# Leaky ReLU as one Prelu on ScalarE, and the third block's probabilities turned by VectorE

## The chip, the cores and the metric

The kernel runs on one core of a Trainium2 chip. The metric is the device time of one execution in microseconds (us), taken as the median of several runs. Five engines work side by side, each with its own list of instructions, done in order: PE (TensorE, matrix products), DVE (VectorE), ACT (ScalarE), POOL (GpSimd) and SP (SyncE, which here only issues DMA transfers). An instruction at the head of a list that waits holds up everything behind it in that list.

## What is computed

Attention over chunks of 64 tokens, then two feed-forward layers with 4608 tokens each; the first has a leaky ReLU, the second a rational function.

```python
# attention: q, k, v are (8, 8, 576, 64); every chunk of 64 tokens for itself
scores = (1 / sqrt(64)) * q_c @ k_c.T
attn = exp(scores - max(scores)); attn = attn / (sum(attn) + 1e-9)
x = (attn @ v_c) as (4608, 512)

# first layer: w_in (512, 2048), w_out (2048, 512)
h = x @ w_in
x = maximum(0.01 * h, h) @ w_out

# second layer
h = x @ w_in2
P = a[0] + a[1]*h + a[2]*h*h + a[3]*h*h*h
Q = 1 + |b[0]| * |h| + |b[1]| * h*h
out = (P / (Q + 1e-6)) @ w_out2
```

## The kernel before

**Tiles.** The 4608 tokens are 9 blocks of 512 (`BLOCKS`); an attention unit `u` is 128 tokens, four units to a block, 36 in all. A step of a layer is a pair (block `i`, slice `f` of 128 of the 2048 hidden columns): `gemm1` makes the 128x512 hidden values in PSUM (`hh`, two buffers), the activation turns them into `gh` and `gl`, and `gemm2` adds their product to four PSUM accumulators (`oa`, `ob`). Values are kept as a high and a low part so that three products give almost the precision of fp32; so each `gemm1` and each `gemm2` is 12 matmuls of 128x512. `gemm2` runs two steps behind `gemm1` (`L1 = 2`).

**Weights.** They come as 64-bit words and are decoded on the chip into the high and low part `w`: two maskings (`a`, lines 260, 261), `re` on ScalarE (265), `t` (269), `sg` (273), `hi` (285), `lo` (291) on VectorE, and `cp` on ScalarE (284). The first layer's are decoded in the start-up, in pieces of 1024 columns (`f` below `WIDE` = 10) and then of 512; the second layer's during the first layer.

**Attention of a unit.** `qk` and `v` load; `S` makes the scores (PE, line 359); `mx` takes the maximum and subtracts it (DVE, 367 and 369); `ex` is Exp (ACT, 376); `nm` sums and scales (DVE, 381 to 387); `T` turns the probabilities (PE against an identity matrix, 403, into PSUM); `p` copies them out (two on ACT, 411); `PV` multiplies with `v` (PE, 420); `xh` and `xl` split the result into high and low part (ACT 431, DVE 429). Scores, turned probabilities and `PV` share the PSUM tile `at` from unit 4 on (`pa` and `pb` for units 0 to 3). In the main loop the turn is done another way: `att_turn` lets VectorE transpose blocks of 32x32 from `e` straight into `pt` (line 395, four instructions for each half of the tile).

**Activation of the first layer.** Three engines' steps: `ta` (ACT, 453) copies 0.01*h out of PSUM into `t`, `tm` (DVE, 458) takes the maximum of that and h, `gh` (ACT, 463) rounds it to the high part, `gl` (DVE, 468) subtracts.

**Order.** The order within each engine is that of the program text; only waits on data move it in time. For the first 32 steps (`NSTART`: 5 of block 0, 16 of block 1, 11 more of block 0) the text order is made by a planner: `start_ops` lists every piece with an engine, an estimated duration and what must precede it, and `ordered` puts them into one list by earliest start and then by due time (`late`). So a number in that table changes the order on every engine, the SP's list of transfers too. Units 8 to 11, the third block's, are made ready in this stretch. After it, from step 32, a plain loop runs, one unit of attention in every four steps; then the second layer.

Of the kernel before, what the change touches and what calls it, by code (L numbers as in the profile page):

```python
# [34 lines left out]
L1, L2 = 2, 3  # L35
WIDE = 10
PIECES = [(f, 0, 2) for f in range(WIDE)] + [(f, h, h + 1) for f in range(WIDE, NF) for h in range(2)]
NPAIR = 4


def start_ops():


    ops, d = [], 0.15

    def op(key, eng, us, *deps, wait=d):
        ops.append((key, eng, us, wait, [k for k in deps if k is not None]))

    last_b1 = SPLIT + NF - 1
    for u in range(13):  # L50
        first = u < NPAIR
        op(("qk", u), "Q", 1.4, ("S", u - 2), wait=2.2)
        op(("S", u), "P", 1.0, ("qk", u), ("xl", u - 2) if first else ("p", u - 1), ("xl", NPAIR - 1) if u == NPAIR else None)
        op(("mx", u), "D", 1.4, ("S", u), ("T", u - 2))
        op(("ex", u), "A", 0.63, ("mx", u))
        op(("nm", u), "D", 1.8, ("ex", u))
        op(("T", u), "P", 1.0, ("nm", u), ("p", u - 1), ("ex", u), ("xl", u - 1) if not first else None)
        op(("p", u), "A", 1.2, ("T", u), ("PV", u - 2) if u < 8 else ("PV", u - 1))
        op(("v", u), "Q", 0.7, ("PV", u - 2), wait=2.2)
        if u == 12:  # L60
            continue
        op(("PV", u), "P", 1.0, ("p", u), ("v", u), ("xl", u - (2 if first else 1)))
        op(("xh", u), "A", 0.6, ("PV", u), ("G1", last_b1) if u >= 8 else None)
        op(("xl", u), "D", 0.69, ("xh", u))
    op(("qk", 13), "Q", 1.4, ("S", 11), wait=2.2)
    for n, (f, a, b) in enumerate(PIECES):
        w = b - a
        ring = 3
        old = n - ring
        if f >= WIDE and PIECES[n - ring][0] < WIDE:  # L70
            old = None
        tail = [("lo", n - 3)]
        if f >= WIDE - 1:
            tail.append(("PV", 7))
        if f >= WIDE:
            tail += [("lo", WIDE - 1 - j) for j in range(3)]
        op(("raw", n), "Q", 1.45 * w, ("lo", old) if old is not None else None, wait=2.2)
        op(("a", n), "D", 0.1 + 0.72 * w, ("raw", n), *tail)
# [3 lines left out]
        op(("hi", n), "D", 0.07 + 0.36 * w, ("sg", n))  # L82
        op(("lo", n), "D", 0.14 + 0.55 * w, ("hi", n), ("t", n))
        op(("cp", n), "A", 0.2 + 0.4 * w, ("sg", n))
    done = {}
    for n, (f, a, b) in enumerate(PIECES):
        for h in range(a, b):
            done[f, h] = ("lo", n)
    for s, (i, f, first, last) in enumerate(STEPS[:NSTART]):
        op(("G1", s), "P", 2.72, done[f, 0], ("cp", done[f, 0][1]), *[("xl", 4 * i + k) for k in range(4)], ("tm", s - 2), ("G1", s - 1))  # L90
        op(("ta", s), "A", 0.6, ("G1", s), ("gl", s - 1))
        op(("tm", s), "D", 0.69, ("ta", s))
        op(("gh", s), "A", 0.63, ("tm", s), ("G2", s - 3))
        op(("gl", s), "D", 0.69, ("gh", s))
        if s < NSTART - L1:
            op(("G2", s), "P", 2.72, done[f, 1], ("gl", s), ("G1", s + L1 - 1), ("G2", s - 1),
               ("fin", s - 1) if first and s else ("xl", NPAIR - 1))
        if last and s < NSTART - 1:
            op(("fin", s), "A", 2.4, ("G2", s))
    return ops  # L100


def ordered(ops, log=None):
# [6 lines left out]
    for s in range(NSTART):  # L110
        late[ix["G1", s]] = 40 + step * s
        if ("G2", s) in ix:
            late[ix["G2", s]] = 40 + step * (s + L1) + 2.7
    for u in (11, 12):
        late[ix["S", u]] = 40 + step * NSTART - 60
    users = [[] for _ in ops]
    for n, dd in enumerate(deps):
        for m in dd:
# [37 lines left out]
def tile_kernel(ctx: ExitStack, tc: tile.TileContext, qt, kt, vt, w1, w2, a, b, out):  # L156
# [172 lines left out]


    ld = {}
    NTURN = 13
    NTWO = 8
    att = {}

    def load_qk(u):
# [26 lines left out]
    def att_max(u, ps):  # L363
        s = ps[:, :, 0:256].rearrange("p j (h t) -> p j h t", h=KC)
        mx = apool.tile([P, 8], F32, tag="mx", name=f"mx{u}")
        e = e0[u % 2] if u < NTWO else apool.tile([P, 8, CH], F32, tag="e", name=f"e{u}", bufs=1)
# [31 lines left out]
    def att_transpose(u, ps):  # L398
        e = att["e", u]
        for h in range(8):  # L400
            for c in range(2):
                r = slice(c * CH, c * CH + CH)
                nc.tensor.matmul(ps[r, c, h * CH:h * CH + CH], e[r, h, :], ident[r, r], start=True, stop=True)  # L403

    def prob_tile(u):
        return p0[u % 2] if u < NTWO else pt
# [43 lines left out]

    def act1a(i, f, ps):
        t = t0pool.tile([P, TM], F32, tag="t0", name=f"t{i}_{f}")[:, :BLOCKS[i]]
        nc.scalar.activation(out=t, in_=ps, func=AF.Copy, scale=0.01)  # L453
        gt[0, i, f] = t, ps

    def act1m(i, f):
        t, ps = gt[0, i, f]
        nc.vector.tensor_tensor(out=t, in0=t, in1=ps, op=ALU.max)  # L458

    def act1b(i, f):  # L460
        t, _ = gt[0, i, f]
# [118 lines left out]
    def start_up():  # L580
# [11 lines left out]
        def fin(s):  # L592
# [21 lines left out]
    with tc.manual_schedule(), tc.tile_pool(name="tpool", bufs=1) as t0pool:  # L614
        with tc.tile_pool(name="apool", bufs=2) as apool, tc.tile_pool(name="rpool", bufs=2) as rpool:
# [16 lines left out]
            for s, (i, f, first, last) in enumerate(STEPS[:-NF]):  # L632
# [137 lines left out]
```

## Time and profile before

| | |
|---|---|
| median of 3 runs | 1689.52 us (1686.84 to 1689.7) |
| the profiled execution, its own time | 1688.19 us |
| its span (first to last instruction) | 1686.2 us |
| PE busy | 1649.6 us, 98% |
| DVE busy | 1260.2 us, 75% |
| ACT busy | 798.0 us, 47% |
| POOL busy | 211.7 us, 13% |

The span is what the engines' rows cover; the own time has 2.0 us more around it. A busy time is a sum over stages with different limits, so a stage is read from rows of its own stretch: how long each engine was busy there, what its idle time waited for, and which clock TensorE was granted (1.00 is its full 2.4 GHz).

### The profile page before, as it was taken

The page shows a single profiled execution, that of the slowest core. Times are in us where ns is not written, and L with a number is a line of the kernel's source. Part 1 is how long each engine was busy: PE and PEld are TensorE (multiplying, and loading weights), DVE is VectorE, ACT ScalarE, POOL GpSimd, SP SyncE. Part 2 cuts the span into 40 slices and gives each one's busy share as a digit, 9 for nine tenths or more (in the row PEclk, how much of TensorE's full clock was granted, in tenths as well). Part 3 has the DMA queues.
Part 4 walks back from the last instruction along what each step waited for, and adds up shares of the span by engine and source line. Part 5 has one row for each costly group of instructions (what it writes and reads, how often), then busy time and mean ns, then how long its engine had stood idle before and what let it go on. Part 6 is the DMA issues. An engine that isn't in the chain of part 4 may idle for free.

```text
span 1686.2 us, 24489 instructions
## 1 busy us (share of the span) xinstructions
PE 1649.6 (98%) x9634; PEld 1356.0 (80%) x9634; DVE 1260.2 (75%) x2081; ACT 798.0 (47%) x1321; POOL 211.7 (13%) x173
## 2 busy tenths in 40 slices
PE   6899999999999999999999999999999999999998
PEld 5687778888888888888887888888888888888886
DVE  7897527666666667766237989898988888888887
ACT  4554423333333333333225655665566656665654
POOL 0000000000000000000002222222222222222221
PEclk9999999999999999999999999999999999999999
DMA  7433113232332332231464010101010101000000
GB/s 287 138 114 107 64 53 119 86 126 95 100 126 94 119 106 96 93 116 60 159 213 141 1 51 1 50 1 50 1 50 1 50 1 48 3 26 26 2 24 25
DMA packets 54259, 127.41 MB, mean 76 GB/s; under 512 B 6272, under 2 KB 6272, under 8 KB 52864
## 3 DMA queue, kind: packets, MB, share of 16 engines
q1 hardware_dynamic: 54144, 125.86, 21.8%
q8 instruction: 75, 1.23, 0.3%
q14 instruction: 40, 0.33, 0.1%
HBM read 89.13 MB, written 36.70 MB: 75 GB/s over the span
## 4 chain that ended last, share of the span: by engine, by line
PE 95%; DVE 3%; ACT 1%; issue 0%; DMA 0%; SPq 0%; ACTq 0%; DVEq 0%
PE hh L444 45%; PE oa L516 23%; PE ob L516 23%; PE at L359 1%; PE at L403 1%; PE at L420 1%; DVE mx L367 0%; ACT ep L411 0%; DMA k<-in_k 0%; DVE ep L369 0%; DVE d L273 0%; DVE ep L387 0%; DVE d L269 0%; DVE x L429 0%; DVE sm L381 0%
## 5 line engine op out<-in xcount | busy, mean ns | idle before, releaser
L444 PE MATMUL hh<-x,w 128*128 128x512 f32 x3456 | 832.8, 390 | 1.4 <-ACT x L431 0.7
L444 PEld LDWEIGHTS hh<-x,w 128*128 128x128 f32 x3456 | 648.9, 188 | 137.4 <-DVE x L429 1.4
L516 PE MATMUL oa<-gh,w 128*128 128x512 f32 x1152 | 406.7, 394 | 0.8 <-ACT gh L499 0.8
L516 PE MATMUL ob<-gh,w 128*128 128x512 f32 x1152 | 402.0, 390 | 0.0
L489 POOL TENSOR_TENSOR u<-u,ah 128x512 f32<-128x512 f32 x144 | 187.0, 1298 | 718.0 <-DVE u L486 718.0
L458 DVE TENSOR_TENSOR t<-t,hh 128x512 f32<-128x512 f32 x144 | 98.9, 687 | 220.3 <-ACT t L453 220.0
L516 PEld LDWEIGHTS oa<-gh,w 128*128 128x128 f32 x1152 | 216.8, 188 | 47.7 <-ACT gh L499 1.6
L516 PEld LDWEIGHTS ob<-gh,w 128*128 128x128 f32 x1152 | 216.6, 188 | 45.4
L453 ACT ACTIVATE t<-hh 128x512 f32<-128x512 f32 x144 | 86.1, 598 | 311.1 <-PE hh L444 283.6
L485 ACT ACTIVATE ah<-hh 128x512 f32<-128x512 f32 x144 | 86.3, 599 | 309.0 <-PE hh L444 308.2
L516 PE MATMUL oa<-gl,w 128*128 128x512 f32 x576 | 225.7, 392 | 2.9 <-DVE gl L500 2.7
L516 PE MATMUL ob<-gl,w 128*128 128x512 f32 x576 | 224.3, 389 | 0.0
L468 DVE TENSOR_TENSOR gl<-t,gh 128x512 fp32r<-128x512 f32 x144 | 99.3, 689 | 45.9 <-ACT gh L463 40.8
L463 ACT ACTIVATE gh<-t 128x512 fp32r<-128x512 f32 x144 | 90.8, 630 | 86.0 <-DVE t L458 85.6
L486 DVE TENSOR_SCALAR u<-ah,absb 128x512 f32<-128x512 f32 x144 | 78.8, 547 | 69.2 <-ACT ah L485 69.2
L516 PEld LDWEIGHTS oa<-gl,w 128*128 128x128 f32 x576 | 108.5, 188 | 26.5 <-DVE gl L500 4.2
L516 PEld LDWEIGHTS ob<-gl,w 128*128 128x128 f32 x576 | 108.4, 188 | 22.7
L387 POOL TENSOR_TENSOR e<-e,sm 128x512 f32<-128x512 f32 x23 | 24.1, 1046 | 740.3 <-DVE sm L383 740.3
L508 DVE SCALAR_TENSOR_TENSOR t<-t,nega,r 128x512 f32<-128x512 f32 x144 | 108.2, 751 | 5.1
L487 ACT ACTIVATE t<-hh,nega 128x512 f32<-128x512 f32 x144 | 111.9, 777 | 0.0
L490 DVE TENSOR_TENSOR t<-t,hh 128x512 f32<-128x512 f32 x144 | 98.8, 686 | 17.3
L491 DVE SCALAR_TENSOR_TENSOR t<-t,nega,hh 128x512 f32<-128x512 f32 x144 | 107.7, 748 | 5.2
(91 smaller groups left out, 1358.6 us busy)
## 6 DMA issues: line engine op xcount, KB each, us to landing
raw<-in_w SPq DMA_DIRECT2D x44, 512.0 KB, 4.6
w<-wd SPq DMA_DIRECT2D x32, 512.0 KB, 4.5
raw<-in_w SPq DMA_DIRECT2D x10, 1024.0 KB, 6.6
q<-in_q SPq DMA_DIRECT2D x36, 256.0 KB, 4.3
k<-in_k SPq DMA_DIRECT2D x36, 256.0 KB, 4.5
v<-in_v SPq DMA_DIRECT2D x36, 256.0 KB, 4.1
x<-xd SPq DMA_DIRECT2D x36, 256.0 KB, 3.5
out_t<-y SPq DMA_DIRECT2D x36, 256.0 KB, 2.4
```

What stands on the lines that cost most here:

```text
L444: nc.tensor.matmul(ps, w[wp][:, 0, kc * P:(kc + 1) * P], x[:, xp, kc, :], start=(kc == 0 and (wp, xp) == (0, 0)), stop=(kc == KC - 1 and ( ...
L453: nc.scalar.activation(out=t, in_=ps, func=AF.Copy, scale=0.01)
L458: nc.vector.tensor_tensor(out=t, in0=t, in1=ps, op=ALU.max)
L463: nc.scalar.activation(out=gh, in_=t, func=AF.Copy)
L468: nc.vector.tensor_tensor(out=gl, in0=t, in1=gh.bitcast(F32), op=ALU.subtract)
L485: S.activation(out=ah, in_=ps, func=AF.Abs)
L487: S.activation(out=t, in_=ps, func=AF.Identity, scale=nega[:, 3:4], bias=nega[:, 2:3])
L489: nc.gpsimd.tensor_tensor(out=u, in0=u, in1=ah, op=ALU.mult)
L490: V.tensor_tensor(out=t, in0=t, in1=ps, op=ALU.mult)
L491: V.scalar_tensor_tensor(out=t, in0=t, scalar=nega[:, 1:2], in1=ps, op0=ALU.add, op1=ALU.mult)
L508: V.scalar_tensor_tensor(out=g0, in0=g0, scalar=nega[:, 0:1], in1=r, op0=ALU.add, op1=ALU.mult)
L516: nc.tensor.matmul(o_acc(dc, n), w[wp][:, 1, dc * P:(dc + 1) * P], g[gp], start=(first and (wp, gp) == (0, 0)), stop=(last and (wp, gp) == ...
```

## The change

`NTURN` is now 8: from unit 8 on (before: 13) the probabilities are turned by VectorE's `att_turn` and go to `pt` without PSUM, TensorE and ScalarE. The leaky ReLU is one ScalarE instruction (`Prelu` with slope 0.01) where it was a scaled copy and a maximum on VectorE; `act1m` is gone in all loops. In the planner's table, `mx` of a unit above 4 must follow `PV` of the unit before, some durations are other numbers, and the due times given for `S` of units 11 and 12 are replaced by due times for `xl` of unit 11 and `p` of unit 12.

```diff
+NTURN = 8
-        op(("S", u), "P", 1.0, ...)
+        op(("S", u), "P", 0.7, ...)
-        op(("mx", u), "D", 1.4, ("S", u), ("T", u - 2))
+        op(("mx", u), "D", 1.4, ("S", u), ("T", u - 2), ("PV", u - 1) if u > NPAIR else None)
-        op(("T", u), "P", 1.0, ("nm", u), ("p", u - 1), ("ex", u), ("xl", u - 1) if not first else None)
-        op(("p", u), "A", 1.2, ("T", u), ("PV", u - 2) if u < 8 else ("PV", u - 1))
+        if u < NTURN:
+            op(("T", u), "P", 1.0, ("nm", u), ("p", u - 1), ("ex", u), ("xl", u - 1) if not first else None)
+            op(("p", u), "A", 1.2, ("T", u), ("PV", u - 2))
+        else:
+            op(("T", u), "D", 1.75, ("nm", u), ("PV", u - 1))
+            op(("p", u), "D", 1.75, ("T", u))
...
-        op(("tm", s), "D", 0.69, ("ta", s))
-        op(("gh", s), "A", 0.63, ("tm", s), ("G2", s - 3))
+        op(("gh", s), "A", 0.63, ("ta", s), ("G2", s - 3))
...
-    for u in (11, 12):
-        late[ix["S", u]] = 40 + step * NSTART - 60
+    late[ix["xl", 11]] = 40 + step * NSTART - 22
+    late[ix["p", 12]] = 40 + step * NSTART - 8
...
     def act1a(i, f, ps):
-        nc.scalar.activation(out=t, in_=ps, func=AF.Copy, scale=0.01)
+        nc.scalar.activation(out=t, in_=ps, func=AF.Prelu, alpha=0.01)
...
-    def act1m(i, f):
-        t, ps = gt[0, i, f]
-        nc.vector.tensor_tensor(out=t, in0=t, in1=ps, op=ALU.max)
...
-            "ex": att_exp, "nm": norm, "T": lambda u: att_transpose(u, at2), "p": lambda u: att_probs(u, at2),
+            "ex": att_exp, "nm": norm, "T": lambda u: att_transpose(u, at2) if u < NTURN else att_turn(u, 0),
+            "p": lambda u: att_probs(u, at2) if u < NTURN else att_turn(u, 1),
```

What the table does to the lists shows at three places. The first is SP's list of transfers at the very start; q, k and v are the units' inputs, raw0_0 is the first piece of weights. Before:

```order
L347 DMA v1_151<-in_v 128x512
L223 DMA raw0_0_153<-in_w1 128x2048
L341 DMA q2_178<-in_q 128x512
L341 DMA k2_180<-in_k 128x512
L341 DMA q3_188<-in_q 128x512
L341 DMA k3_190<-in_k 128x512
L223 DMA raw0_1_213<-in_w1 128x2048
```

After:

```order
L349 DMA v1_151<-in_v 128x512
L343 DMA q2_156<-in_q 128x512
L343 DMA k2_158<-in_k 128x512
L343 DMA q3_179<-in_q 128x512
L343 DMA k3_181<-in_k 128x512
L227 DMA raw0_0_189<-in_w1 128x2048
L227 DMA raw0_1_215<-in_w1 128x2048
```

The first piece of weights now stands behind the loads of units 2 and 3, whose buffers come free with S of units 0 and 1.

The second place is VectorE's list around unit 6 in the front (mx6 is the maximum, sm6 the sums, x0_1 the split x of block 1, d0_4 the weight piece in decoding, t and gl the activation of a step). Before:

```order
L458 TENSOR_TENSOR t0_1_617<-t0_1_617,hh1_76 128x512
L367 TENSOR_REDUCE mx6_682<-at_80 128x8
L369 TENSOR_TENSOR ep_114<-at_80,mx6_682 128x512
L273 SCALAR_TENSOR_TENSOR d0_4_642<-raw0_4_444,d0_4_642 128x1024
L381 TENSOR_REDUCE sm6_709<-ep_114 128x8
L382 TENSOR_SCALAR sm6_709<-sm6_709 128x8
L383 RECIPROCAL sm6_709<-sm6_709 128x8
L387 TENSOR_TENSOR ep_114<-ep_114,sm6_709 128x512
L429 TENSOR_TENSOR x0_1_123<-at_80,x0_1_123 128x2x4x64
L468 TENSOR_TENSOR gl0_0_1_686<-t0_1_617,gh0_0_1_685 128x512
```

After:

```order
L369 TENSOR_REDUCE mx6_684<-at_80 128x8
L371 TENSOR_TENSOR ep_114<-at_80,mx6_684 128x512
L431 TENSOR_TENSOR x0_1_123<-at_80,x0_1_123 128x2x4x64
L277 SCALAR_TENSOR_TENSOR d0_4_640<-raw0_4_502,d0_4_640 128x1024
L383 TENSOR_REDUCE sm6_708<-ep_114 128x8
L384 TENSOR_SCALAR sm6_708<-sm6_708 128x8
L385 RECIPROCAL sm6_708<-sm6_708 128x8
L389 TENSOR_TENSOR ep_114<-ep_114,sm6_708 128x512
L466 TENSOR_TENSOR gl0_0_1_645<-t0_1_614,gh0_0_1_644 128x512
```

The maximum of the activation (line 458) is gone, and xl of unit 5 stands before the sums of unit 6, no longer behind them.

The third place is TensorE's list in the third block, around units 9 and 10 (k, q: scores; pt, v: PV; ident: turn; hh and oa, ob: the steps' products). Before:

```order
L359 MATMUL at_80<-k10_927,q10_925 64x64 x16
L420 MATMUL at_80<-pt_113,v9_922 64x64 x16
L444 MATMUL hh1_76<-x0_0_124,w0_5_772 128x512 x12
...
L403 MATMUL at_80<-ident_95,e10_1715 64x64 x16
L444 MATMUL hh0_75<-x0_0_124,w0_6_844 128x512 x12
L359 MATMUL at_80<-k11_1602,q11_1600 64x64 x16
L420 MATMUL at_80<-pt_113,v10_1619 64x64 x16
```

After:

```order
L422 MATMUL at_80<-pt_113,v9_917 64x64 x16
L361 MATMUL at_80<-k10_923,q10_921 64x64 x16
L446 MATMUL hh1_76<-x0_0_124,w0_9_1088 128x512 x12
...
L446 MATMUL hh0_75<-x0_0_124,w0_10_1169 128x512 x12
...
L422 MATMUL at_80<-pt_113,v10_1711 64x64 x16
L361 MATMUL at_80<-k11_1731,q11_1729 64x64 x16
```

The turns against the identity matrix are gone from TensorE, PV of a unit now precedes S of the next, and the pair stands later, with two whole steps (two gemm1, two gemm2) from one pair to the next.

## Rows read from the trace of the kernel before

**Rows 1.** Stretches: us, busy (count) of PE, PEld, DVE, ACT, POOL; clock, DMA, GB/s.

```profile
0.00:85.00 85.00, 62.04 (x913) 48.88 (x914) 68.78 (x107) 40.76 (x57) 0.70 (x6) 0.96 0.60 214
85.00:155.00 70.00, 70.00 (x311) 57.90 (x309) 64.40 (x110) 35.12 (x55) 0.00 (x0) 1.00 0.33 112
155.00:200.00 45.00, 40.38 (x474) 31.93 (x476) 27.48 (x50) 21.71 (x37) 0.00 (x0) 1.00 0.26 85
200.00:250.00 50.00, 48.56 (x296) 39.95 (x287) 14.85 (x24) 12.46 (x21) 0.00 (x0) 1.00 0.09 27
250.00:860.00 610.00, 610.00 (x4059) 501.62 (x4058) 387.30 (x732) 207.04 (x349) 24.05 (x23) 1.00 0.33 112
```

**Rows 2.** TensorE's waits: total us, times, longest us.

```profile
PE at L420 <- DVE e L369: 4.6, 3, 1.5
```

**Rows 3.** Timeline of TensorE, third block: start us, us, what, [idle before <-releaser].

```profile
162.03 0.69 PE L359 MATMUL at<-k,q 64*64 64x64 f32 x32
164.26 0.69 PE L420 MATMUL at<-pt,v 64*64 64x64 f32 x32 [1.54 <-DVE e L369]
164.89 3.01 PE L444 MATMUL hh<-x,w 128*128 128x512 f32 x12
...
170.55 1.15 PE L403 MATMUL at<-ident,e 64*64 64x64 f32 x32
171.63 0.50 PE L516 MATMUL oa<-gh,w 128*128 128x512 f32 x1
```

**Rows 4.** Timeline of TensorE, one pair of S and PV in the main loop.

```profile
273.31 0.69 PE L359 MATMUL at<-k,q 64*64 64x64 f32 x32
...
274.40 0.50 PE L516 MATMUL oa<-gh,w 128*128 128x512 f32 x1
```

**Rows 5.** Timeline of TensorE, end of the start-up.

```profile
244.07 0.69 PE L420 MATMUL at<-pt,v 64*64 64x64 f32 x32
246.21 1.15 PE L403 MATMUL at<-ident,e 64*64 64x64 f32 x32 [1.44 <-DVE x L429]
247.28 3.01 PE L444 MATMUL hh<-x,w 128*128 128x512 f32 x12
```

**Rows 6.** Timeline of TensorE, the start of step 5.

```profile
84.57 5.51 PE L444 MATMUL hh<-x,w 128*128 128x512 f32 x23 [0.70 <-DVE x L429]
```

**Rows 7.** Timeline of VectorE in the front.

```profile
16.92 0.68 DVE L429 TENSOR_TENSOR x<-pa,x 128x512 fp32r<-128x512 f32 x1
...
67.81 0.68 DVE L458 TENSOR_TENSOR t<-t,hh 128x512 f32<-128x512 f32 x1
68.41 0.69 DVE L260 TENSOR_SCALAR d<-raw 128x1024 int32<-128x1024 int32 x1
...
82.69 1.22 DVE L273 SCALAR_TENSOR_TENSOR d<-raw,d 128x1024 int32<-128x1024 int32 x1
83.83 0.68 DVE L429 TENSOR_TENSOR x<-at,x 128x512 fp32r<-128x512 f32 x1
```

**Rows 8.** Timeline of SP's transfers at the start; issue, duration of the issue.

```profile
8.87 0.91 SPq L223 DMA_DIRECT2D raw<-in_w  x2
```

**Rows 9.** Line 223 between 8 and 9.4 us: issue to landing.

```profile
DMA to landing us min/median/max: 6.9/8.4/9.9
```

**Rows 10.** Timeline of VectorE in the main loop: one half of a turn.

```profile
263.77 1.77 DVE L395 STREAM_TRANSPOSE pt<-e 32x256 f32<-32x256 f32 x4
```

**Rows 11.** Timeline after S of unit 12: TensorE's next row, VectorE's scaled probabilities.

```profile
200.32 3.02 PE L444 MATMUL hh<-x,w 128*128 128x512 f32 x12
...
203.73 0.69 DVE L387 TENSOR_TENSOR e<-e,sm 128x512 f32<-128x512 f32 x1
```

**Rows 12.** Groups of instructions on the page: busy us, mean ns, idle before and its releaser.

```profile
L458 DVE TENSOR_TENSOR t<-t,hh 128x512 f32<-128x512 f32 x144 | 98.9, 687 | 220.3 <-ACT t L453 220.0
L453 ACT ACTIVATE t<-hh 128x512 f32<-128x512 f32 x144 | 86.1, 598 | 311.1 <-PE hh L444 283.6
L487 ACT ACTIVATE t<-hh,nega 128x512 f32<-128x512 f32 x144 | 111.9, 777 | 0.0
```

More of the change, by code (lines that the diff above doesn't have):

```diff
@@ L52, in start_ops @@
         op(("qk", u), "Q", 1.4, ("S", u - 2), wait=2.2)
-        op(("S", u), "P", 1.0, ("qk", u), ("xl", u - 2) if first else ("p", u - 1), ("xl", NPAIR - 1) if u == NPAIR else None)
-        op(("mx", u), "D", 1.4, ("S", u), ("T", u - 2))
+        op(("S", u), "P", 0.7, ("qk", u), ("xl", u - 2) if first else ("p", u - 1), ("xl", NPAIR - 1) if u == NPAIR else None)
+        op(("mx", u), "D", 1.4, ("S", u), ("T", u - 2), ("PV", u - 1) if u > NPAIR else None)
         op(("ex", u), "A", 0.63, ("mx", u))
         op(("nm", u), "D", 1.8, ("ex", u))
-        op(("T", u), "P", 1.0, ("nm", u), ("p", u - 1), ("ex", u), ("xl", u - 1) if not first else None)
-        op(("p", u), "A", 1.2, ("T", u), ("PV", u - 2) if u < 8 else ("PV", u - 1))
+        if u < NTURN:
[4 more added lines that the diff above has]
+            op(("p", u), "D", 1.75, ("T", u))
         op(("v", u), "Q", 0.7, ("PV", u - 2), wait=2.2)
@@ L61, in start_ops @@
             continue
-        op(("PV", u), "P", 1.0, ("p", u), ("v", u), ("xl", u - (2 if first else 1)))
+        op(("PV", u), "P", 0.7, ("p", u), ("v", u), ("xl", u - (2 if first else 1)))
         op(("xh", u), "A", 0.6, ("PV", u), ("G1", last_b1) if u >= 8 else None)
@@ L77, in start_ops @@
         op(("raw", n), "Q", 1.45 * w, ("lo", old) if old is not None else None, wait=2.2)
-        op(("a", n), "D", 0.1 + 0.72 * w, ("raw", n), *tail)
+        op(("a", n), "D", 0.14 + 0.62 * w, ("raw", n), *tail)
         op(("re", n), "A", 0.2 + 0.4 * w, ("a", n))
@@ L81, in start_ops @@
         op(("sg", n), "D", 0.14 + 0.55 * w, ("re", n))
-        op(("hi", n), "D", 0.07 + 0.36 * w, ("sg", n))
+        op(("hi", n), "D", 0.15 + 0.27 * w, ("sg", n))
         op(("lo", n), "D", 0.14 + 0.55 * w, ("hi", n), ("t", n))
@@ L89, in start_ops @@
     for s, (i, f, first, last) in enumerate(STEPS[:NSTART]):
-        op(("G1", s), "P", 2.72, done[f, 0], ("cp", done[f, 0][1]), *[("xl", 4 * i + k) for k in range(4)], ("tm", s - 2), ("G1", s - 1))
+        op(("G1", s), "P", 2.72, done[f, 0], ("cp", done[f, 0][1]), *[("xl", 4 * i + k) for k in range(4)], ("ta", s - 2), ("G1", s - 1))
         op(("ta", s), "A", 0.6, ("G1", s), ("gl", s - 1))
-        op(("tm", s), "D", 0.69, ("ta", s))
-        op(("gh", s), "A", 0.63, ("tm", s), ("G2", s - 3))
+        op(("gh", s), "A", 0.63, ("ta", s), ("G2", s - 3))
         op(("gl", s), "D", 0.69, ("gh", s))
@@ L96, in start_ops @@
             op(("G2", s), "P", 2.72, done[f, 1], ("gl", s), ("G1", s + L1 - 1), ("G2", s - 1),
-               ("fin", s - 1) if first and s else ("xl", NPAIR - 1))
+               ("fin", s - 1) if first and s else ("xl", NPAIR - 1), ("xl", NPAIR - 2))
         if last and s < NSTART - 1:
@@ L331, in tile_kernel @@
     ld = {}
-    NTURN = 13
-    NTWO = 8
     att = {}
@@ L365, in att_max @@
         mx = apool.tile([P, 8], F32, tag="mx", name=f"mx{u}")
-        e = e0[u % 2] if u < NTWO else apool.tile([P, 8, CH], F32, tag="e", name=f"e{u}", bufs=1)
+        e = e0[u % 2] if u < NTURN else apool.tile([P, 8, CH], F32, tag="e", name=f"e{u}", bufs=1)
         V.tensor_reduce(out=mx.rearrange("p (j h) -> p j h", j=2), in_=s, axis=AX.X, op=ALU.max)
@@ L405, in prob_tile @@
     def prob_tile(u):
-        return p0[u % 2] if u < NTWO else pt
+        return p0[u % 2] if u < NTURN else pt
     def att_probs(u, ps):
@@ L452, in act1a @@
         t = t0pool.tile([P, TM], F32, tag="t0", name=f"t{i}_{f}")[:, :BLOCKS[i]]
-        nc.scalar.activation(out=t, in_=ps, func=AF.Copy, scale=0.01)
-        gt[0, i, f] = t, ps
-    def act1m(i, f):
-        t, ps = gt[0, i, f]
-        nc.vector.tensor_tensor(out=t, in0=t, in1=ps, op=ALU.max)
+        nc.scalar.activation(out=t, in_=ps, func=AF.Prelu, alpha=0.01)
+        gt[0, i, f] = t
     def act1b(i, f):
-        t, _ = gt[0, i, f]
+        t = gt[0, i, f]
         gh, gl = (gpool.tile([P, TM], F32R, tag=g, name=f"{g}0_{i}_{f}")[:, :BLOCKS[i]] for g in ("gh", "gl"))
@@ L605, in start_up @@
             "lo": lambda n: decode_lo(0, n),
-            "G1": g1, "ta": lambda s: act1a(*STEPS[s][:2], hp[s]), "tm": lambda s: act1m(*STEPS[s][:2]),
+            "G1": g1, "ta": lambda s: act1a(*STEPS[s][:2], hp[s]),
             "gh": lambda s: act1b(*STEPS[s][:2]), "gl": lambda s: act1c(*STEPS[s][:2]),
@@ L651, in tile_kernel @@
                 act1a(i, f, ps)
-                act1m(i, f)
                 if r == 0:
@@ L682, in tile_kernel @@
                 act1a(i, f, ps)
-                act1m(i, f)
                 act1b(i, f)
```

## The prediction

> **What bounds the kernel now.** First I read the busy times by stretch [rows 1]. From 250 to 860 us TensorE is busy all 610 us, at full clock, while VectorE has 387 of 610: there a lighter VectorE or ScalarE gives nothing. TensorE's holes lie ahead of 250: 23 us (85 less 62.0) up to 85, none from 85 to 155, 4.6 in the third block (155 to 200), 1.4 from 200 to 250. In the front VectorE is the dense engine, 68.8 of 85 busy; it decodes weights and works for attention at once. In the third block it has 27.5 of 45. So there are two different limits: in the front VectorE's list in order, from 85 to 250 TensorE's own list. Second, TensorE's waits [rows 2]: in the third block three, 4.6 us in all, PV of a unit held until the maximum of the next unit has read the shared tile `at`. Third, TensorE's timeline there [rows 3], which shows what an attention unit costs between the steps' products, and the same in the main loop, where the turn is already on VectorE [rows 4].
>
> So I ask two things: when does the unbroken run of TensorE begin (now 84.57, step 5 [rows 6]), and how much of TensorE's list between it and the main loop (247.28, its first gemm1 [rows 5]) goes.
>
> **The change part by part.**
>
> *Third block, S and PV.* From S of unit 9 at 162.03 to the next gemm1 at 164.89 pass 2.86 us [rows 3]. The same pair without a wait takes 1.09 in the main loop (273.31 to 274.40) [rows 4]. In the new list PV of a unit comes before S of the next, so PV no longer waits for that unit's maximum; the maximum waits for PV instead, on VectorE. Three pairs (units 8 with 9, 9 with 10, 10 with 11): 3 x 1.77 = 5.3 us. What is queued behind the waiting maximum on VectorE is xl of the unit before, then the sums, and the `gl` of a step; TensorE needs that `gl` two steps later, so this stays covered.
>
> *Third block, turns.* A turn on TensorE takes 1.08 us (170.55 to 171.63) [rows 3]. Units 8 to 11: 4 x 1.08 = 4.3 us. The one of unit 12 stands at the end: from PV of unit 11 at 244.07 to the first gemm1 of the main loop at 247.28 are 3.21 us, with a wait of 1.44 for xl and the turn [rows 5]. PV alone is half a pair, 0.55; so 2.7 us go. VectorE takes on two halves of 1.77 per unit [rows 10], 5 x 3.54 = 17.7 us, and ScalarE loses the copies. VectorE's cover: 17.5 us idle in 155 to 200 and 35 in 200 to 250 [rows 1], and it sheds 27 maxima (steps 5 to 31) of 0.60 in the same time, 16 us (67.81 to 68.41, from one instruction to the next [rows 7]). One turn (unit 8) falls into the dense stretch 85 to 155, where VectorE has 5.6 us idle and sheds 12 x 0.60. If that cover were gone, 1 us too much on VectorE would be 1 us at the next gemm1 that needs a weight.
>
> The third block by these rows: 5.3 + 4.3 + 2.7 = 12.3 us off TensorE's list. Bounds: nothing of the waits gained, 7.0; edges at each switch between 64x64 and 128x512 products also gained, some 0.2 for each of five turns, 13.3.
>
> The Trainium skill weighs against this part: "VectorE: DVE Perf Modes", Rules for kernel authors, gives a full 128x128 transpose to TensorE if it may land in PSUM, and VectorE's to 32x32 blocks. Here the turn is of 64x64 blocks, so by that rule units 8 to 12 would stay on TensorE and the sum would be about 5.4 us smaller; the rows say that TensorE is the full engine here, and VectorE, dearer by the piece, has room.
>
> *Front.* TensorE's run can begin when xl of unit 7 (83.83 [rows 7]) is done. Counted in VectorE's list ahead of it: tm of steps 0 to 4 are gone, 5 x 0.60 = 3.0; `sg` of weight 6 now stands behind it, 1.1 (82.69 to 83.83 [rows 7]); `hi` and `lo` of weight 5 now stand ahead, 0.6 + 1.1. Together 2.4 us less work.
>
> Beside the work there are VectorE's waits in the front, 16.2 us of 85 [rows 1]. Two moves change them. For the better: xl of unit 5 stands before the sums of unit 6, so that the turn of unit 6 no longer waits for it, and S behind PV in units 4 to 7 lets the split of a unit start at once; each later unit's maximum then comes about 1 us earlier. For the worse: the first weights are queued on SP behind the loads of units 2 and 3, which wait for S of units 0 and 1. They are issued where now the second and third piece are, at 8.87 [rows 8], with 6.9 to 9.9 us to landing there [rows 9], thus at 15.8 to 18.8. VectorE's masking of them, two instructions of 0.60, stands ahead of xl of unit 0, which is at 16.92 now and can't be earlier by much [rows 7], since it waits for that unit's PV. So landing by 15.7 costs nothing and landing at 18.8 costs 3.1. There is one transfer of 1 MB less ahead of it than the second piece has now, so I take the near end, nothing. The list also decodes weight 1 later than now (gemm1 of step 1 waits for it and the turn of unit 4 stands behind that); I count this against part of the gain. I take 0.9 us for the waits together, between a loss of 3.1 and a gain of 3.4. The gain's end is from the clock: over the first 85 us it was 0.96 of full [rows 1], so 3.4 us were lost at the lower level, 1.2 GHz, after waits; shorter waits may save all of it or nothing.
>
> Front: 2.4 + 0.9 = 3.3 us. The run would begin at about 81.
>
> *Prelu.* It replaces a copy with a scale from the same PSUM tile, 598 ns on ScalarE. Its cost isn't in this trace; below, that copy; above, the activation with two tensor operands for scale and bias, 777 ns [rows 12]. I take 0.6, the nearest: also one input, one constant. At 0.18 us more, ScalarE (23 us idle or more in each stretch from 85 on) hides it; in the front it could cost 5 x 0.18 = 0.9. The maximum that goes, 687 ns [rows 12], gives 0.60 in the front and nothing from 250 on, where TensorE is full.
>
> The skill speaks against this too: "ScalarE: Activation LUTs", Rules for kernel authors, puts relu and max on VectorE. The rows show that the pass over PSUM on ScalarE is paid already, so the rule would only keep the maximum; by it the front's 3.0 us fall out of the sum.
>
> *Sum.* 12.3 + 3.3 = 15.6 us. The profiled execution took 1688.2 (span 1686.2 and 2.0 around it), so 1672.6. The median of the three runs is 1.3 us above that execution and the lowest 1.3 below, so I leave it there: 1672.5.
>
> **The rivals.**
>
> A. *The front gives nothing*: the first weights land at 18.8, or weight 1 holds TensorE. For it: the row of landings, and VectorE's strict order. Against: 2.4 us of work are gone for certain. 12.3 remain: 1676.
>
> B. *The half-clock stretches of the front vanish too*: 3.4 us more, about 1669. For it: the turn of unit 6 starts earlier. Against: TensorE still waits for every unit's sums in the front, and VectorE would soon be the limit again.
>
> C. *The new chain on VectorE is late for PV.* From the end of S of unit 12 (200.32, the next product's start) to its scaled probabilities (203.73 + 0.69) are 4.1 us [rows 11]; two halves of the turn make it 7.6, xl and a gl of 0.6 each 8.9. From one pair to the next the new list has four products of 2.7 us, 10.9. That leaves 2 us. ScalarE copies the accumulators out (four copies) just behind PV of unit 8, ahead of that unit's split; such a thing uses the 2 us up. With 1.5 us of wait for four units: 6 us back, 1678.5.
>
> D. *Slower than before*: the same chain, PV of units 9 to 12, but each wait over 15.6 / 4 = 3.9 us; that is from a chain of 14.8 us on. It needs 6 us of foreign work between S and the turn on VectorE, that is more than one whole weight piece in each gap. At 5 us a unit: 1693. Against: VectorE is 39% idle in the third block [rows 1], and the planner's list has few weight pieces left there.
>
> E. *It doesn't do what it says*: the freed time is taken by another wait at the same steps (a weight not yet decoded, as VectorE carries the turn of unit 8 in the dense stretch), 1688.
>
> **How the numbers follow.** The forecast 0.62 with a range of its own from 1669 to 1676; A 0.14; B 0.08; C 0.09; D 0.03; E 0.04. The range for 8 in 10: it takes in the third block between 7 and 13.3 and the front between 0 and 6.7 (3.3 and 3.4), without both worst ends at once: 1667 to 1680. Within 0.2% (3.4 us) this measurement can't tell from no change. Faster by more: all but D, E and a rest of C, 0.92; within: most of E, 0.04; slower: D and a part of E, 0.04.
>
> **What would show it.** Right: the first long run of TensorE begins at about 81; the first gemm1 of the main loop at 231 to 232; no row of TensorE's turn with `e` as input, no wait of PV for VectorE's subtraction (line 371 in the new text); the activation row of ScalarE at about 600 ns; two loads of function tables, as before; from 250 on TensorE's steps in the same rhythm. Wrong: PV of units 9 to 12 waiting for the transposes (C, D); gemm1 in 100 to 180 waiting for a `w` (E); VectorE waiting for a transfer near 13 to 18 us and the run beginning at 84 or later (A); the clock at 1.00 all through the front (B).

## The result and the profile after

| | before | changed |
|---|---|---|
| median of the comparison | 1689.38 us (4 runs) | 1674.45 us (1673.56 to 1676.48, 4 runs) |
| the profiled execution, its own time | 1688.19 us | 1673.93 us |
| its span | 1686.2 us | 1672.1 us |
| PE, DVE, ACT busy | 1649.6, 1260.2, 798.0 us | 1641.2, 1183.6, 792.4 us |

The ratio is 0.9919 with a 95% interval of 0.9908 to 0.9931: 14.9 us faster by the medians, 14.1 by the spans. The forecast was 1672.5. First the busy times by stretch, with the columns of [rows 1]:

```profile
0.00:85.00 85.00, 61.93 (x918) 48.88 (x919) 67.33 (x104) 40.64 (x57) 0.70 (x6) 0.98 0.61 216
85.00:155.00 70.00, 70.00 (x310) 57.97 (x309) 63.00 (x110) 38.36 (x61) 0.00 (x0) 1.00 0.32 115
155.00:200.00 45.00, 45.00 (x316) 36.96 (x316) 23.80 (x47) 15.09 (x26) 0.00 (x0) 1.00 0.18 59
200.00:250.00 50.00, 50.00 (x396) 40.63 (x395) 29.16 (x58) 15.36 (x26) 1.05 (x1) 1.00 0.28 96
250.00:860.00 610.00, 610.00 (x4001) 501.66 (x4000) 310.65 (x614) 206.75 (x348) 23.01 (x22) 1.00 0.34 112
```

The holes of TensorE in the third block and behind it (4.6 and 1.4 us [rows 1]) are gone: it is busy all the time from 85 to 860. The first stretch still has 23 us of holes. From 250 on VectorE lost 77 us of work and nothing came of it, since TensorE was full there already.

TensorE's timeline in the third block, to compare with [rows 3] (start us, duration, what, [idle before <-releaser]):

```profile
178.50 0.69 PE L422 MATMUL at<-pt,v 64*64 64x64 f32 x32
179.01 0.65 PE L361 MATMUL at<-k,q 64*64 64x64 f32 x32
179.59 3.02 PE L446 MATMUL hh<-x,w 128*128 128x512 f32 x12
```

PV of one unit and S of the next take 1.09 us from the start of the one to the next product, as in the main loop [rows 4]; no wait, and no turn with `e` as input stands in TensorE's list from unit 8 on. The two marks of the forecast, the begin of the unbroken run and the first gemm1 of the main loop [rows 5, 6], are now

```profile
83.30 5.51 PE L446 MATMUL hh<-x,w 128*128 128x512 f32 x23 [0.46 <-DVE x L431]
...
233.03 2.88 PE L446 MATMUL hh<-x,w 128*128 128x512 f32 x12
```

Before, 247.28 less 84.57 = 162.71 us lay between them; now 149.73. So the third block gave 12.98 us (12.3 were forecast), and the front 84.57 less 83.30 = 1.27 (3.3 were forecast). The span's 14.1 are these two, within 0.2.

VectorE's timeline in the front, to compare with [rows 7]:

```profile
16.76 0.69 DVE L264 TENSOR_SCALAR d<-raw 128x1024 int32<-128x1024 int32 x1 [3.76 <-DMA raw<-in_w]
17.97 0.68 DVE L431 TENSOR_TENSOR x<-pa,x 128x512 fp32r<-128x512 f32 x1
...
59.94 0.69 DVE L369 TENSOR_REDUCE mx<-at 128x8 f32<-128x512 f32 x1 [2.90 <-ACT x L433]
...
82.56 0.69 DVE L431 TENSOR_TENSOR x<-at,x 128x512 fp32r<-128x512 f32 x1 [0.86 <-PE at L361]
```

VectorE stands idle for 3.76 us until the first weights land, xl of unit 0 comes 1.05 us later than before (17.97 for 16.92), and then VectorE waits again for the split of a unit (`xh`, line 433) before the next unit's maximum. The chain of waits of this execution has the transfer in it:

```profile
8.90 7.83 DMA raw<-in_w
16.76 0.69 DVE d L264
18.05 0.61 DVE x L431
```

Last the page's group of the Prelu, which answers to the copy in [rows 12]: the same 598 ns.

```profile
L455 ACT ACTIVATE t<-hh 128x512 f32<-128x512 f32 x144 | 86.2, 598 | 407.7 <-PE hh L446 399.0
```

### The profile page after: what moved, and what is told of

Its sections match the earlier page's. It is cut to its first block, busy times and chain, and to the rows that moved or that the text cites. A ratio compares the mean times of both kernels' runs of the same rounds, so it can differ in the third digit from the quotient of the medians.

```text
span 1672.1 us, 24047 instructions
## 1 busy us (share of the span) xinstructions
PE 1641.2 (98%) x9474; PEld 1350.2 (81%) x9474; DVE 1183.6 (71%) x1977; ACT 792.4 (47%) x1311; POOL 211.8 (13%) x173
## 4 chain that ended last, share of the span: by engine, by line
PE 96%; DVE 2%; ACT 1%; DMA 1%; issue 0%; SPq 0%; DVEq 0%; ACTq 0%
PE hh L446 46%; PE oa L514 24%; PE ob L514 23%; PE at L361 1%; PE at L422 1%; DMA raw<-in_w 0%; PE at L405 0%; DMA k<-in_k 0%; DVE x L431 0%; ACT ep L413 0%; DVE d L277 0%; ACT x L433 0%; DVE ep L371 0%; DVE mx L369 0%; DVE r L505 0%
## 5 line engine op out<-in xcount | busy, mean ns | idle before, releaser
L483 ACT ACTIVATE ah<-hh 128x512 f32<-128x512 f32 x144 | 86.3, 599 | 309.7 <-PE hh L446 308.8
L488 DVE TENSOR_TENSOR t<-t,hh 128x512 f32<-128x512 f32 x144 | 98.9, 687 | 17.0
L502 ACT ACTIVATE l<-u,cst 128x512 f32<-128x512 f32 x144 | 103.3, 717 | 0.0
L505 DVE SCALAR_TENSOR_TENSOR r<-r,l 128x512 f32<-128x512 f32 x144 | 99.6, 692 | 5.0
```

Source lines behind the costliest of these rows:

```text
L483: S.activation(out=ah, in_=ps, func=AF.Abs)
L488: V.tensor_tensor(out=t, in0=t, in1=ps, op=ALU.mult)
L502: S.activation(out=l, in_=u0, func=AF.Abs_reciprocal_sqrt, bias=cst[:, 0:1])
L505: V.scalar_tensor_tensor(out=r, in0=r, scalar=2.0, in1=l, op0=ALU.subtract, op1=ALU.mult)
```

## The experiments

The theory after the result: the third block's gain is the turns and the waits between S and PV, each worth what the prediction gave it; the front gave little because VectorE waits there, so that less work on it only makes it wait longer. The rivals: the third block's gain comes from the list as a whole; or the front's term was right and something else took it back. Each kernel below is the changed one with one edit. Where an order is edited, `ahead(a, b)` moves piece `a` directly before `b` in the start-up's list.

**The turns back on TensorE** (`turn_pe`).

```diff
-        if u < NTURN:
+        if u < 13:
             op(("T", u), "P", 1.0, ...)
-            op(("p", u), "A", 1.2, ("T", u), ("PV", u - 2))
+            op(("p", u), "A", 1.2, ("T", u), ("PV", u - 2) if u < 8 else ("PV", u - 1))
...
-            "T": lambda u: att_transpose(u, at2) if u < NTURN else att_turn(u, 0),
+            "T": lambda u: att_transpose(u, at2) if u < 13 else att_turn(u, 0),
...
```

> The changed kernel, but the turns of units 8 to 12 are again products on TensorE with ScalarE's copies (the planner makes its list for that). Theory (the turns were paid on TensorE's full list): 5 turns of 1.08 us and the edges around them come back, 5.4 to 6.7 us, so about 1680.5; the run of TensorE still begins at 83.3. Rival (the gain came from the new order alone, the turns were beside other work): 1674 to 1675, no change against the changed kernel.

Measured: 1678.85 us (5 runs), ratio to before 0.9952 (0.9940 to 0.9965). Its timeline of TensorE:

```profile
190.91 1.15 PE L405 MATMUL at<-ident,e 64*64 64x64 f32 x32
191.99 3.02 PE L446 MATMUL hh<-x,w 128*128 128x512 f32 x12
...
238.48 1.75 PE L446 MATMUL hh<-x,w 128*128 128x512 f32 x7
```

Its run begins at 82.21, so 156.27 us lie between the marks, 6.54 more than in the changed kernel, with no wait of TensorE between. Five turns: 1.31 each, the 1.08 of [rows 3] and 0.23 for the edges to the 128x512 products. VectorE, freed of the transposes, gave nothing back: it was not the limit. The spans differ by less than the marks, 4.7 us: this run began 1.09 us earlier, and from VectorE's last copy to the end it took 3.6 us where the changed kernel took 4.4.

**The maximum ahead of PV again** (`mx_first`).

```diff
+        for u in (8, 9, 10):
+            ahead(("S", u + 1), ("PV", u))
+            ahead(("mx", u + 1), ("PV", u))
```

> The changed kernel, but for units 9, 10 and 11 the scores and the maximum stand ahead of PV of the unit before, as in the kernel before. Theory (PV waited because the next unit's maximum, ahead of it in the order, still read the shared tile): three waits of 1.5 us or a little more come back as PV waiting for VectorE's subtraction, 4.6 to 5.4 us, so about 1679.5. Rival (the waits went because PV now stands later and its probabilities are ready): no wait, 1674.5.

Measured: 1677.37 us (5 runs), ratio 0.9945 (0.9932 to 0.9957). TensorE's timeline and its row of waits:

```profile
177.06 0.69 PE L361 MATMUL at<-k,q 64*64 64x64 f32 x32
179.30 0.69 PE L422 MATMUL at<-pt,v 64*64 64x64 f32 x32 [1.54 <-DVE e L371]
179.92 3.01 PE L446 MATMUL hh<-x,w 128*128 128x512 f32 x12
```

```profile
PE at L422 <- DVE e L371: 4.6, 3, 1.5
```

The old wait is back to the digit [rows 2, 3]. From the begin of the run (81.87) to the main loop (236.91) are 155.04 us: 5.31 more, 3 x 1.77.

**S ahead of PV, the maximum behind it** (`s_first`).

```diff
+        for u in (8, 9, 10):
+            ahead(("S", u + 1), ("PV", u))
```

> The changed kernel with S of units 9 to 11 ahead of PV of the unit before, as in the old list, but the maximum of the next unit still behind PV in the program. Theory (what made PV wait was the maximum reading the shared tile ahead of it in the program, not the order of S and PV): no wait of PV for VectorE's subtraction, first gemm1 of the main loop 149.5 to 150 us behind the begin of the run, as in the changed kernel. Rival (the wait comes with S ahead of PV): three waits of about 1.5 us and some 155 us from one to the other.

TensorE's timeline:

```profile
179.84 0.69 PE L361 MATMUL at<-k,q 64*64 64x64 f32 x32
180.36 0.65 PE L422 MATMUL at<-pt,v 64*64 64x64 f32 x32
180.94 3.02 PE L446 MATMUL hh<-x,w 128*128 128x512 f32 x12
```

No wait, and 149.73 us from 84.65 to 234.38. So it is not the order of S and PV that counts but where the maximum, VectorE's reader of the shared tile, stands against PV. The one time, 1675.17 us, goes with a late front (below).

**The maximum of the activation back** (`tm_back`).

```diff
-        nc.scalar.activation(out=t, in_=ps, func=AF.Prelu, alpha=0.01)
+        nc.scalar.activation(out=t, in_=ps, func=AF.Copy, scale=0.01)
...
+        nc.vector.tensor_tensor(out=t, in0=t, in1=ps, op=ALU.max)
```

> The changed kernel with its list, but the leaky ReLU is a scaled copy and VectorE's maximum again, the maximum just ahead of gh. Theory (VectorE's work in the front sets the start of TensorE's run): 5 maxima of 0.60 us, the run begins 3.0 us later, at 86.3, and nothing is lost after it: about 1677.5. Rival 1 (VectorE has waits enough in the front, 17.7 of 85 us, that hide them): 83.3 to 84, 1674.5 to 1675. Rival 2 (VectorE is then too full between 85 and 155 for the decoding and the turn of unit 8): waits of gemm1 for a weight, over 1679.

Measured: 1676.7 us (5 runs), ratio 0.9935 (0.9923 to 0.9948). VectorE's timeline:

```profile
56.95 0.68 DVE L460 TENSOR_TENSOR t<-t,hh 128x512 f32<-128x512 f32 x1
59.98 0.69 DVE L369 TENSOR_REDUCE mx<-at 128x8 f32<-128x512 f32 x1 [1.23 <-ACT x L433]
...
70.94 0.69 DVE L369 TENSOR_REDUCE mx<-at 128x8 f32<-128x512 f32 x1 [0.77 <-ACT x L433]
```

The maxima of units 6 and 7 stand at 59.98 and 70.94, where the changed kernel has 59.94 and 70.90 with longer waits before them (2.90 and 1.36 us). The extra instructions go into VectorE's idle time. What they do cost shows in the distances: 11.40 us from the maximum of unit 5 to that of unit 6, where executions without them and at full clock have 10.95; 10.96 to unit 7, as without; from there to the run's begin 13.43 for 12.40. That is some 1.5 us, not 5 x 0.60, so the run's begin lies between the theory's 86.3 and the rival's 83.3 to 84; the distance from unit 4 to unit 5, 12.02 for 10.59, has a stretch at the lower clock in it and is left out. Another such stretch lies behind the run's begin, where the first 23 products take 6.87 us for 5.51. Counted from the first masking, with one stretch ahead of the run's begin in each, it is 67.92 us for 66.54, thus 1.38 by this other way. The copy's group on the page has 597 ns:

```profile
L455 ACT ACTIVATE t<-hh 128x512 f32<-128x512 f32 x144 | 85.9, 597 | 290.2 <-PE hh L446 279.6
```

**The same kernel again** (`after_again`).

> The changed kernel once more, to have its time from the same chip as the runs beside it and a second profile of its front. Theory (the start of TensorE's run moves from execution to execution with the landing of the first weights: 14.98 to 16.76 us in four executions, begin of the run 81.9 to 83.3): it lands anywhere between and the run begins 66.5 to 67 us behind it. Rival (the front is set by its list and the 83.3 of the first profile comes again whenever the weights land).

Measured: 1675.6 us (1673.37 to 1678.32, 5 runs), ratio 0.9926 (0.9913 to 0.9938). The run began at 85.00, 67.4 us behind the first masking: neither the theory's 66.5 to 67 nor the rival's 83.3, and later than the 84.57 of the kernel before. So the begin of the run moves from one execution of the same front to the next. `turn_pe`, `mx_first` and `s_first` leave the front's list as it is, so there are five executions of it; times in us, from VectorE's and TensorE's timelines:

| execution | first masking | maximum of unit 5, 6, 7 | run begins | main loop |
|---|---|---|---|---|
| before | 12.89 | 46.45, 59.18, 71.92 | 84.57 | 247.28 |
| changed | 16.76 | 47.45, 59.94, 70.90 | 83.30 | 233.03 |
| after_again | 17.63 | 47.78, 60.06, 72.57 | 85.00 | 234.73 |
| turn_pe | 15.40 | 46.32, 58.82, 69.79 | 82.21 | 238.48 |
| mx_first | 14.98 | 46.00, 56.94, 69.46 | 81.87 | 236.91 |
| s_first | 14.74 | 45.93, 58.47, 72.22 | 84.65 | 234.38 |
| raw_first | 13.16 | 46.64, 57.61, 70.14 | 82.57 | 232.31 |
| raw_mid | 14.70 | 46.70, 59.20, 70.14 | 82.56 | 232.30 |
| s8_first | 15.55 | 46.31, 58.81, 69.76 | 81.82 | 231.53 |
| g2_early | 17.20 | 47.73, 59.08, 70.44 | 82.84 | 232.58 |
| combo | 14.11 | 46.05, 57.40, 68.74 | 80.76 | 230.49 |
| combo_again | 13.52 | 46.60, 57.95, 69.29 | 81.31 | 231.04 |

Two things make the spread. One is the landing: the first masking comes between 14.74 and 17.63 in the five executions of one front. The other is the clock. One unit's maximum follows the last by 10.95 us where the granted clock is 1.00, by 12.5 where the ten microseconds around hold a stretch at the lower level (1.2 GHz), and by 13.75 in `s_first`, where the stretch is longer. The rows of such ten microseconds, of the changed kernel and of `s_first`:

```profile
50.00:60.00 10.00, 7.49 (x112) 6.05 (x113) 6.99 (x12) 5.00 (x7) 0.00 (x0) 0.83 0.34 109
```

```profile
60.00:70.00 10.00, 7.23 (x47) 5.75 (x46) 7.95 (x12) 4.94 (x7) 0.00 (x0) 0.66 0.36 143
```

So one such stretch costs 1.55 us, the long one 2.8. The kernel before had two between units 5 and 7 (12.73 and 12.74 apart), the changed one had one. It has no execution without them, but TensorE's timeline gives their price there too. First the kernel before, from a turn to the next S; then the changed one at full clock, from a turn to the next PV, with the same gemm2 between:

```profile
64.44 1.15 PE L403 MATMUL at<-ident,ep 64*64 64x64 f32 x32 [2.46 <-DVE x L429]
...
70.06 0.69 PE L359 MATMUL at<-k,q 64*64 64x64 f32 x32
```

```profile
65.00 1.15 PE L405 MATMUL at<-ident,ep 64*64 64x64 f32 x32 [2.77 <-DVE ep L389]
...
69.04 0.69 PE L422 MATMUL at<-ep,v 64*64 64x64 f32 x32
```

That is 5.62 for 4.04, 1.58 more, and 1.52 at the other one (52.32 to 57.88). Without these stretches, an estimate from these distances, the run would begin at 81.5 before and at 81.75 in the profiled execution after: at equal clock, and with the weights landing at 16.76, the new front is not shorter. In `turn_pe` and `mx_first`, where they landed by 15.4, the same reckoning gives 80.7 and 80.3.

Most of the stretches follow a wait of TensorE for a turn. Ten executions (all but `tm_back`, `g2_early` and the two `combo`) have a wait of 2.5 to 3.6 us ahead of the turn of unit 5 and another ahead of that of unit 6. At 14 of these 20 waits a stretch begins in the wait or within 1.5 us behind it; at six it doesn't, as at 65.00 in the changed kernel.

**The first weights earlier** (`raw_first`, `raw_mid`).

```diff
+        ahead(("raw", 0), ("qk", 2))    # raw_first
+        ahead(("raw", 0), ("qk", 3))    # raw_mid
```

> The changed kernel, but the first piece of weights is issued ahead of q and k of unit 2, as before. Theory (the late landing at 16.7 us cost about 1 us, since VectorE's xl of unit 0 came at 17.97 where it was at 16.92): VectorE's wait of 3.8 us for the transfer goes, xl of unit 0 is at 16.5 to 17.0, and the run begins about 1 us earlier, at 82.3; 1673.4. Rival (a later wait takes it, S of unit 3 or the split of unit 3 at 35.1 us): the run begins at 83.2 or later, 1674.4.

> The changed kernel, but the first piece of weights is issued between the loads of unit 2 and those of unit 3, thus at about 6.4 us where it was 8.9, and not beside the loads of unit 1 either. Theory (VectorE's wait for the weights is what sets the front's start, 1 for 1): landing at 13 to 14.5 us, xl of unit 0 at 16.0 to 16.7, the run begins at 81.5 to 82.5; on average 1 us less, 1673.4. Rival (xl of unit 3 at 34 to 35 us waits for its xh anyway, so this ends there): 1674.4.

Measured: 1673.18 us (5 runs), 0.9915 (0.9902 to 0.9929), and 1673.97 (4 runs), 0.9917 (0.9904 to 0.9931). By time neither can be told from the changed kernel. In the profiles xl of unit 0 comes at 16.69 and 16.73, as early as before the change, but no earlier: it then waits for its unit's `xh` (2.25 and 0.73 us). So the late landing costs up to the 1.05 us of the profiled execution, and no more is to be had there.

**Links further down the chain** (`s8_first`, `g2_early`, `mx567`).

```diff
+        ahead(("S", 8), ("xh", 7))              # s8_first
...
+        for s in (0, 1):                        # g2_early
+            ahead(("gl", s), ("sg", s + 3))
+            ahead(("G2", s), ("T", s + 5))
...
+        for u in (5, 6, 7):                     # mx567
+            ahead(("mx", u), ("xh", u - 1))
```

> The changed kernel, but S of unit 8 stands ahead of xh of unit 7 in the order. Theory (S of unit 8 waits 0.7 us for xh of unit 7, as both use the shared tile, and xl of unit 7, which releases the run, waits for S): the wait of S goes, the run begins 0.5 to 0.8 us earlier against the weights' landing; 1673.8 where the changed kernel has 1674.45. Rival (xh then waits for S, so xl comes no earlier): the same, and the time too.

> The changed kernel, but gl and gemm2 of steps 0 and 1 stand ahead of the turns of units 5 and 6 (they stood behind them, while TensorE waited 2.8 us for each turn). Theory (VectorE's idle time in the front comes from attention's chain, turn, copy, PV, xh, next maximum, which has gemm2 in the middle on TensorE): the maximum of unit 6 comes 2 to 3 us earlier (57 where it was 59.9), the waits of 2.8 go, the run begins 2 us or more earlier; about 1672.3. Rival (VectorE's work alone sets the front): the idle time shows up elsewhere in VectorE's list and the run begins as before; 1674.4.

> The changed kernel with the maximum of units 5 to 7 back ahead of the split (xh) of the unit before, as in the old list. Theory (the new place of the maximum in the front delays it by the wait for the split's neighbours, 0.8 us at unit 6: 59.94 against 59.18, and gives the time back at xl): the maximum of unit 6 counted from the first masking comes 0.5 to 1 us earlier than in the changed kernel (42.75 to 43.2 us behind it there), but PV then waits for the maximum again, so that the begin of the run is within 0.7 us of the changed kernel's 66.5 behind the masking. Rival (the new place is a gain of about 1 us per unit, as the prediction put it): the begin of the run moves to 68 to 70 behind the masking.

`s8_first`: 1673.92 us (5 runs), 0.9920 (0.9907 to 0.9934). S of unit 8 no longer waits, but the next product does, 0.72 us for the same `xh`; from the maximum of unit 7 to the run's begin are 12.06 us for 12.40. `g2_early`: 1672.84 us (4 runs), 0.9910 (0.9897 to 0.9924). The waits for turns fall by some 5 us, but others come up for all of it: a wait of 2.8 us becomes one of 1.3 for ScalarE's copy and one of 1.6 for `gl`. TensorE's rows of waits, first of the changed kernel, then of the version with all moves, `combo`, which has the same ones:

```profile
PE at L405 <- DVE ep L389: 10.8, 4, 3.4
...
PE at L422 <- ACT ep L413: 1.3, 1, 1.3
```

```profile
PE at L405 <- DVE ep L389: 6.1, 4, 3.4
PE at L422 <- ACT ep L413: 3.9, 3, 1.3
PE oa L514 <- DVE gl L466: 3.4, 3, 1.6
```

The distances of the maxima in `g2_early` are 11.35 and 11.36, longer than the 10.95 at full clock without the move, and the maximum of unit 6 came at 59.08, not at the expected 57. Yet the clock stayed at 1.00 all through the front, so no 1.55 was lost. `mx567`: one run, 1677.23. VectorE's timeline:

```profile
60.29 0.69 DVE L369 TENSOR_REDUCE mx<-at 128x8 f32<-128x512 f32 x1 [3.56 <-PE at L361]
...
62.43 0.69 DVE L431 TENSOR_TENSOR x<-at,x 128x512 fp32r<-128x512 f32 x1 [0.72 <-ACT x L433]
```

The maximum now waits for S, and xl for `xh` behind it. Both expectations missed: the maximum came 0.8 us later behind the masking, not earlier, and the run began at 87.35, later than either said. It went the rival's way and past it (71.1 behind the masking for 68 to 70). But the clock was lower in this front (0.84 over 85 us), in two stretches nearly as long as that of `s_first`. If each cost the 2.8 us of that one, an estimate, the run would begin at 81.7, as the changed kernel's would at full clock. So whether the order of maximum and split holds a microsecond per unit, as the prediction had it, stays open with this one execution.

**All three moves** (`combo`, `combo_again`): `raw_mid`, `s8_first` and `g2_early` in one list.

```diff
+        ahead(("raw", 0), ("qk", 3))
+        ahead(("S", 8), ("xh", 7))
+        for s in (0, 1):
+            ahead(("gl", s), ("sg", s + 3))
+            ahead(("G2", s), ("T", s + 5))
```

> Three re-orderings of the changed kernel's start-up list at once: first weights' load between the loads of units 2 and 3, S of unit 8 ahead of xh of unit 7, gl and gemm2 of steps 0 and 1 ahead of the turns of units 5 and 6. Theory (the front is a chain of waits behind the landing of the first weights, and each move takes one link out of it): begin of the unbroken run of TensorE behind the first masking 66.5 us in the changed kernel, 65.6 with the gemm2 move, 66.3 with the S8 move; together 65 to 65.5. With the masking at 14.7 to 15.5 as the middle place of the load gives, the run begins at 80 to 81, the first gemm1 of the main loop at 230 to 231, and the time is 1671 to 1672.5. Rival (VectorE's own work is the limit there, waits only move): run begin at 82 to 82.5 as with each move alone, 1673 to 1674.

> The version with the three moves in the start-up list once more, unchanged. Theory (the lower clock of TensorE in the front follows its long waits for a turn, and the moved gl and gemm2 fill these): granted clock 1.00 in every 10 us from 40 to 100, the maxima of units 5, 6 and 7 11.3 to 11.4 us apart as in the first execution (46.05, 57.40, 68.74), the unbroken run of TensorE beginning 12.0 us behind the last of them, at 80.5 to 81.5; 1671 to 1673 us. Rival (the clock falls by chance of the execution, and the two executions with these moves were lucky): a stretch at 0.83 between 40 and 90, one distance of about 12.9, the run beginning at 82 to 83.

Measured: 1672.03 us (1671.24 to 1672.26, 4 runs), 0.9899 (0.9882 to 0.9916); again 1671.68 (1671.37 to 1671.83, 4 runs), 0.9905 (0.9888 to 0.9921). VectorE's and TensorE's timelines of the second:

```profile
57.95 0.69 DVE L369 TENSOR_REDUCE mx<-at 128x8 f32<-128x512 f32 x1 [1.75 <-ACT x L433]
...
69.29 0.69 DVE L369 TENSOR_REDUCE mx<-at 128x8 f32<-128x512 f32 x1 [1.75 <-ACT x L433]
```

```profile
81.31 5.51 PE L446 MATMUL hh<-x,w 128*128 128x512 f32 x23 [0.22 <-DVE x L431]
```

The clock was 1.00 in every ten microseconds from 40 to 100 in both, the maxima 11.35 and 11.34 apart, the run 12.02 behind the last: as the theory had it. Of the executions with these moves, `g2_early` and the two `combo`, none has a stretch at the lower level between 40 and 90; each of the other eleven has at least one. This fits a clock that falls behind the long waits for a turn, which these moves split, but it is not shown: in `tm_back` it fell twice behind waits of 1.4 us at most, and not behind one of 3.24. One yardstick of the expectation fell: 65 to 65.5 us from the first masking to the run. It was 66.65, presumably since with weights landing early the chain no longer starts at the masking. All eight times lie below every time of the changed kernel as it stands (1673.37 at the least), so this list is the fastest version here by its medians; the intervals of the ratios still overlap, and one run of `raw_first` took 1670.9.

## Why the prediction was right, and where it was not

*Third block, S and PV: right.* 5.3 us forecast, 5.31 when undone. The reason was right too: `s_first` shows that only the maximum's place counts.

*Third block, turns and the end: right, a little low.* 4.3 and a part of 2.7 for the turns; five turns are 6.54 when undone. The upper bound had the edges, 0.2 for each turn, and they are there. What the two experiments leave of the 12.98 is 1.13 us. It stands where 1.44 of waiting for xl at the end are gone [rows 5], but no run undid that part alone. VectorE's cover held: 23.80 us busy of 45 in the third block with the transposes in it, and no wait of PV, so rivals C and D fell.

The Trainium skill's rule in "VectorE: DVE Perf Modes", Rules for kernel authors, which leaves the full 128x128 transpose to TensorE, would have cost what `turn_pe` shows, 6.5 us, if it is taken for these blocks too: with blocks of 64 and TensorE full, the engine that has room is the right one.

*Prelu: right in its price.* 598 ns, the copy's own. In the main loop the maximum that went gave nothing, as forecast.

*Front: the sum was mis-sized*, 3.3 us forecast for 1.27 in the profiled pair, and by three steps. The first is "tm of steps 0 to 4 are gone, 5 x 0.60 = 3.0": the prediction counted work in a list that has 16.2 us of waits in it, and named those waits itself. Undone, the five cost 1.5; the rest of them went where VectorE waits for `xh` anyway. The second is "I take the near end, nothing" for the landing of the first weights: in the profiled execution they let VectorE go at 16.76, not by 15.7, and xl of unit 0 came 1.05 us later. (That xl could not come much earlier than 16.92 isn't in [rows 7], where it stands right behind a decoding; `raw_first` shows it, with its wait of 2.25 us for `xh`.) The third is the 0.9 for shorter waits: the maximum of unit 6 came at 59.94, not about a microsecond earlier than 59.18. With the 0.6 for the decoding that moved ahead, the parts are 1.5 less 0.6 less 1.05, or about -0.15 at full clock, where the estimate from the table gives -0.25; one stretch less at the lower level, 1.55, makes up the rest of the measured 1.27. So the front gave nothing, as rival A had it (by a landing of 16.76, not of 18.8), and of the two stretches at the lower clock one went, where rival B had both go. That is luck of the pair: in `after_again`, with two stretches again and a later landing, the run began 0.43 us later than in the kernel before. The total came out near because the third block gave 0.7 more, the front 2 less, and the 1.27 of the front came from the clock.

*The clock.* The prediction's bound "shorter waits may save all of it or nothing" was the right form: the same list had one stretch or more in different executions, and the one with the moved gemm2 had none. The Trainium skill, in "TensorE: Matmul & The Clock Gate", section "HAM oscillation — how this bites in real kernels", says that waits inside a loop send the clock down again and again, and that the loop should be rebuilt so that TensorE stays busy. Most executions here agree: the granted clock fell at 14 of 20 waits of some 3 us, and from 40 us on it stayed at 1.00 in the three executions where each was split into two of 1.3 to 1.6; `tm_back`, with two stretches behind shorter waits, does not.

## What to carry to other kernels

Count work taken off an engine only as far as that engine is not waiting in the same stretch: a list with 16 us of waits in 85 gave back half of what left it, while on TensorE's own full list every microsecond counted (11.85 of 12.98 us found again piece by piece). When several engines share a tile, look for the reader that stands ahead of the next writer in the program: moving that one instruction was worth three waits. And when a start-up list moves a transfer past others, take its landing as a spread and compare fronts over several executions, since one pair can differ by the clock alone.

## What the runs showed of the hardware

The first weights' landing varied by 2.9 us over five executions of one list (first masking from 14.74 to 17.63). A stretch of TensorE at the lower level cost 1.55 us where TensorE and VectorE wait for each other in turn, and nothing where VectorE was the limit: from the maximum of unit 3 to that of unit 4 it was 11.97 us in the changed kernel, at 1.00, and 11.97 in `turn_pe`, with 0.58 and 0.57 in the two rows from 20 to 40 us. Prelu and the scaled copy took the same 598 and 597 ns on a 128x512 tile.
